# Squaring a softmax sum on ScalarE instead of GpSimd in a fused attention and SoLU feed-forward kernel

## The chip, the cores and the metric

One core of a Trainium2 chip runs the whole program. The metric is the device time of one execution in microseconds (us). A core has five engines with an instruction queue each: TensorE (PE in the profile, with its weight loads shown as PEld), VectorE (DVE), ScalarE (ACT), GpSimd (POOL) and SyncE (SP), which here only issues transfers.

## The reference

Two stages, with every product in float32. `q` is 4 x 12288 x 128; `kv` is 4 x 384 x 32 x 128 and is averaged over 4 x 4 blocks to 768 keys for each batch.

```python
kv_flat = kv_pool.reshape(B, -1, C) @ w_sr          # keys and values: 768 x 128
s = scale * (q @ k.transpose(0, 2, 1)); s = s - s.max(-1, keepdims=True)
a = np.exp(s); a /= a.sum(-1, keepdims=True) + 1e-09
x = a @ v                                           # tokens x 128
h = x @ w_in                                        # tokens x 1024
e = np.exp(h - h.max(-1, keepdims=True))
solu = h * (e / (e.sum(-1, keepdims=True) + 1e-09))
mu, var = solu.mean(-1), ((solu - mu) ** 2).mean(-1)
out = ((solu - mu) / np.sqrt(var + 1e-06) * g_ln) @ w_out
```

## The kernel before

The 49,152 tokens are 384 tiles of 128 (96 tiles to a batch), and four tiles make a group, so there are 96 groups. One loop runs over slots; slot `s` starts tile `s` and carries on older tiles at fixed distances, so that every engine's queue holds work of several tiles. From slot 9 to slot 389 the order of the instructions on each engine is the order in which the code writes them.

For tile `t` in its own slot `t`: TensorE makes the scores (L359) one slot ahead, VectorE takes the row maximum (L375), ScalarE takes the exponential (L376) and writes its float16 high part (L378), VectorE the low part (L386), and SyncE's queue issues a transposing transfer into `pT` (L389). A group's values are then multiplied (L412), read by ScalarE (L421, L422), and GpSimd makes the low part `xl` (L428). Ten slots behind, at `i = slot - 10`: TensorE makes `h` (L455), VectorE its maximum (L461), ScalarE the second exponential with its sum `z2` (L476). A slot later, for tile `i - 1`: VectorE makes `u` (L490), ScalarE the sum of squares `v3` (L521), GpSimd splits `u` into two float16 parts (L507, L508), and SyncE's queue issues the transposing transfer into `uT` (L513), which the output product (L540) reads two slots later. The scores and `h` share three PSUM buffers, so that TensorE's next scores (L359) wait for VectorE's `u`, and its next `h` for VectorE's low part of the scores.

Once for a group, in slot 4g + 15, `final_scale` makes the factor of the group's rows, (z2'^2 + v3)^(-1/2) for four tiles in one 128 x 4 tile, with z2' = (z2 + 1e-9) times a factor of the batch, `bb[:, 1:2]`. In that slot its code stands after ScalarE's L376 and L378 (tile `slot`) and before ScalarE's L521 (tile `slot - 11`) and GpSimd's L507 and L508 (the same tile). VectorE uses the factor two slots later (L564).

GpSimd has other work for a group: `ql` (L345), `xl` (L428), a sum (L435) whose reciprocal is VectorE's (L440), and, in the first three batches, the pooling of the next batch's keys: 30 additions of 128 x 384 (L201) in the slots 9 to about 67 of a batch, one to every second slot. In the rest of those batches a short series of steps makes the next batch's keys and values. The last batch has none of this. `kv_bound` runs once for a batch and fills `bb`.

Of the kernel before, what the change touches and what calls it, by code (L numbers as in the profile page):

```python
# [11 lines left out]
F32 = mybir.dt.float32  # L12
# [5 lines left out]
AF = mybir.ActivationFunctionType  # L18
ALU = mybir.AluOpType
# [33 lines left out]
def kernel(  # L53
# [15 lines left out]
    nc = tc.nc  # L69
# [52 lines left out]
    state = {}  # L122

    def kv_alloc(b):
        for n, w, dt, bufs in (
            ("kT", NK, F32, 1),
            ("ks", NK, F32, 1),
            ("kh", NK, F32R, 2),
            ("kl", NK, F32R, 2),
            ("ksq", NK, BF16, 1),  # L130
            ("kss", 2, F32, 1),
            ("knm", 2, F32, 1),
            ("vf", NK, F32, 1),
            ("sv", 2, F32, 2),
            ("bb", 2, F32, 2),
        ):
            state[n, b] = bat.tile([P, w], dt, tag=n, name=f"{n}_{b}", bufs=bufs)
        for n in ("vh", "vl"):
            state[n, b] = bat.tile([P, NKC, P], F16, tag=n, name=f"{n}_{b}")
# [125 lines left out]
    def kv_bound(b, part):  # L265

        knm, bb = state["knm", b], state["bb", b]
        if part == 0:
            nc.vector.tensor_tensor(bb[:, 0:1], knm[:, 0:1], knm[:, 1:2], op=ALU.max)
            nc.vector.tensor_scalar(  # L270
                bb[:, 0:1], bb[:, 0:1], wmax2, 1e-20, op0=ALU.mult, op1=ALU.max
            )
            nc.gpsimd.tensor_tensor(bb[:, 0:1], bb[:, 0:1], mhalf[:, 0:1], op=ALU.pow)
        else:
            nc.vector.tensor_scalar(
                bb[:, 1:2], bb[:, 0:1], SC * 1e-3 * 2.0**15, None, op0=ALU.mult
            )
            nc.vector.tensor_scalar(bb[:, 0:1], bb[:, 0:1], SC, None, op0=ALU.mult)

    def kv_vs(b, half):  # L280
        nc.scalar.activation(
            half_of("ks", b, half), half_of("kT", b, half), AF.Copy, scale=state["sv", b][:, 0:1]
        )
# [264 lines left out]
    def final_scale(g):  # L548

        b = g * GT // TPB  # L550
        f = grp.tile([P, GT], F32, tag="f", name=f"f_{g}")
        f2 = grp.tile([P, GT], F32, tag="f2", name=f"f2_{g}")
        nc.gpsimd.tensor_scalar(  # L553
            f, state.pop(("z2", g)), 1e-9, state["bb", b][:, 1:2], op0=ALU.add, op1=ALU.mult
        )
        nc.gpsimd.tensor_tensor(f2, f, f, op=ALU.mult)  # L556
        nc.gpsimd.tensor_tensor(f, f2, state.pop(("v3", g)), op=ALU.add)  # L557
        nc.gpsimd.tensor_tensor(f2, f, mhalf[:, :GT], op=ALU.pow)  # L558
        state["f", g] = f2
# [35 lines left out]
    nc.scalar.dma_start(wsr, w_sr)  # L595
    nc.scalar.mul(w_sr16, wsr, 1.0 / RR)
    kv_alloc(0)
    kv_first(0, (0, 1))
    raw_in = dmt.tile([P, 2 * DFF], I32, tag="pT", name="raw_in")
# [89 lines left out]
    def kv_norms(half):  # L689
# [9 lines left out]
        5: [w_center, partial(kv_norm_max, 0, 0)],  # L699
        6: [partial(kv_norm_max, 0, 1)],  # L700
        7: [w_square, partial(kv_bound, 0, 0)],
        8: [w_norm, partial(kv_bound, 0, 1)],
        9: [w_pow],
        10: [w_high],
# [17 lines left out]
        (93, 0, kv_norm_pe, kv_norm_out), (96, 0, kv_norm_max),  # L722
        (97, 1, kv_norm_pe, kv_norm_out), (99, 1, kv_norm_max),
        (103, 0, kv_bound), (104, 1, kv_bound),
    ]
    WITH_PE = {slot for slot, _, *fs in PLAN if len(fs) > 1}
# [15 lines left out]
    for slot in range(NT + LO + 2):  # L742
# [10 lines left out]
        if ti == 12 and tb + 1 < B:  # L753
            kv_alloc(tb + 1)
# [10 lines left out]
        at_last(slot - NORM, values_norm)  # L765
        at_last(slot - XSP - 1, values_split)
        at_last(slot - FSC, final_scale)
        if slot < NT and 0 < qs < slot and (slot - 1 - qs) % GT == 0:
            q_low(slot // GT + 1)
# [63 lines left out]
```

## Time before, and how its profile is read

| | us |
|---|---|
| median of the 3 runs | 1951.87 |
| lowest and highest run | 1951.87, 1959.1 |
| the profiled execution | 1954.76 |
| its span, first to last instruction | 1953.0 |

The span is what the views of the trace are drawn from; 1.76 us of the profiled execution lie around it. Five engines are each busy for 90% or more of the span. So a share of busy time alone doesn't tell which of them sets the pace: it has to be read stage by stage, from the gaps.

### The profile page before, as it was taken

The page shows a single profiled execution, that of the slowest core. Times are in us where ns is not written, and L with a number is a line of the kernel's source. Part 1 is how long each engine was busy: PE and PEld are TensorE (multiplying, and loading weights), DVE is VectorE, ACT ScalarE, POOL GpSimd, SP SyncE. Part 2 cuts the span into 40 slices and gives each one's busy share as a digit, 9 for nine tenths or more (in the row PEclk, how much of TensorE's full clock was granted, in tenths as well). Part 3 has the DMA queues.
Part 4 walks back from the last instruction along what each step waited for, and adds up shares of the span by engine and source line. Part 5 has one row for each costly group of instructions (what it writes and reads, how often), then busy time and mean ns, then how long its engine had stood idle before and what let it go on. Part 6 is the DMA issues. An engine that isn't in the chain of part 4 may idle for free. (4 is left out here: it accounts for less than half of the span.)

```text
span 1953.0 us, 43521 instructions
## 1 busy us (share of the span) xinstructions
PE 1899.8 (97%) x15678; PEld 1487.8 (76%) x15678; DVE 1797.4 (92%) x2573; ACT 1783.9 (91%) x3141; POOL 1760.0 (90%) x1579
## 2 busy tenths in 40 slices
PE   7999999999999999999999999999999999999997
PEld 4677777777777777777777777777777887787775
DVE  7899999999999999999999999899999999999985
ACT  3998999999999999999999999999999999999995
POOL 3699999999899999999989999999988898988886
PEclk8999999999999999999999999999999999999998
DMA  6899999999999999999999999999999999999996
GB/s 237 174 237 233 235 225 238 221 221 217 213 242 231 238 228 226 226 223 222 217 221 237 237 235 229 228 229 219 223 210 215 223 218 221 225 215 219 224 198 135
DMA packets 1484311, 432.88 MB, mean 222 GB/s; under 512 B 1405889, under 2 KB 1471553, under 8 KB 1483841
## 3 DMA queue, kind: packets, MB, share of 16 engines
q1 hardware_dynamic: 1469840, 410.10, 104.6%
q10 hardware_dynamic: 14256, 20.00, 3.9%
q8 instruction: 125, 2.05, 0.5%
q14 instruction: 90, 0.73, 0.1%
HBM read 52.50 MB, written 25.17 MB: 40 GB/s over the span
## 5 line engine op out<-in xcount | busy, mean ns | idle before, releaser
L508 POOL TENSOR_TENSOR uhl<-u,uhl 128x1024 f16<-128x1024 f32 x384 | 823.2, 2144 | 37.4 <-ACT uhl L505 6.0
L540 PEld LDWEIGHTS <-uT 128*128 128x128 f16 x9216 | 517.5, 98 | 112.8 <-issue 104.6
L540 PE MATMUL o<-wch,uT 128*128 128x128 f16 x6144 | 582.9, 220 | 7.2 <-DMA uT<-uhl 6.8
L540 PE MATMUL o<-wcl,uT 128*128 128x128 f16 x3072 | 536.0, 219 | 0.0
L490 DVE SCALAR_TENSOR_TENSOR u<-h,rz,e 128x1024 f32<-128x1024 f32 x384 | 490.2, 1277 | 24.9 <-ACT e L476 24.5
L461 DVE TENSOR_REDUCE nm<-h 128x1 f32<-128x1024 f32 x384 | 468.9, 1221 | 19.0 <-PE h L455 11.7
L476 ACT ACTIVATE e<-h,nm,rz 128x1024 f32<-128x1024 f32 x384 | 460.1, 1198 | 3.6 <-DVE rz L440 2.8
L521 ACT ACTIVATE junk<-u,su 128x1024 bf16<-128x1024 f32 x384 | 438.0, 1141 | 1.9 <-DVE u L490 1.9
L507 POOL TENSOR_SCALAR uhl<-u 128x1024 f16<-128x1024 f32 x378 | 395.9, 1047 | 10.4 <-DVE u L490 10.2
L412 PE MATMUL xa<-pT,vh 128*128 128x512 f16 x1152 | 391.5, 382 | 7.4 <-DMA pT<-phl 5.2
L375 DVE TENSOR_REDUCE nm<-s 128x1 f32<-128x768 f32 x384 | 365.3, 951 | 34.6 <-PE s L359 34.0
L376 ACT ACTIVATE s<-s,nm 128x768 f32<-128x768 f32 x384 | 335.7, 874 | 60.9 <-DVE nm L375 60.0
L386 DVE SCALAR_TENSOR_TENSOR phl<-s,phl 128x768 f16<-128x768 f32 x384 | 364.9, 951 | 20.0 <-ACT phl L378 10.5
L378 ACT ACTIVATE phl<-s 128x768 f16<-128x768 f32 x384 | 311.4, 811 | 12.0
L455 PE MATMUL h<-w_in_h,xh 128*128 128x512 f32 x768 | 304.9, 478 | 7.0 <-DVE phl L386 3.2
L359 PE MATMUL s<-kh,qh 128*128 128x384 f32 x768 | 264.4, 425 | 7.2 <-DVE u L490 2.8
L455 PE MATMUL h<-w_in_h,xl 128*128 128x512 f32 x768 | 245.1, 400 | 12.0 <-POOL xl L428 11.6
L455 PE MATMUL h<-w_in_l,xh 128*128 128x512 f32 x768 | 240.3, 394 | 0.0
L412 PE MATMUL xa<-pT,vl 128*128 128x512 f16 x576 | 219.1, 380 | 0.0
L359 PE MATMUL s<-kh,ql 128*128 128x384 f32 x768 | 196.2, 337 | 0.0
L359 PE MATMUL s<-kl,qh 128*128 128x384 f32 x768 | 196.1, 336 | 0.0
L455 PEld LDWEIGHTS h<-w_in_h,xh 128*128 128x128 f32 x768 | 140.4, 190 | 72.6 <-issue 18.2
(119 smaller groups left out, 2223.0 us busy)
## 6 DMA issues: line engine op xcount, KB each, us to landing
qf<-in_q_dram SPq DMA_DIRECT2D x96, 256.0 KB, 3.3
out_dram<-ob SPq DMA_DIRECT2D x96, 256.0 KB, 2.8
kv<-in_kv_dram ACTq DMA_DIRECT2D x96, 192.0 KB, 3.1
kv<-in_kv_dram SPq DMA_DIRECT2D x16, 384.0 KB, 7.8
pT<-phl SPq DMA_TRANSPOSE x384, 4.0
uT<-uhl SPq DMA_TRANSPOSE x384, 4.3
raw_in<-in_moe_w_in_dram ACTq DMA_DIRECT2D x1, 1024.0 KB, 6.5
raw_out<-in_moe_w_out_dram SPq DMA_DIRECT2D x1, 1024.0 KB, 7.6
```

Source lines behind the costliest of these rows:

```text
L359: nc.tensor.matmul(s[:, half, :384], lh[:, ts], rh[:, half * 384 : (half + 1) * 384], start=n == 0, stop=n == 2,)
L375: nc.vector.tensor_reduce(nm, s, axis=AX.XY, op=ALU.max, negate=True)
L386: nc.vector.scalar_tensor_tensor(phl[:, 1], state.pop(("s", t)), SC, phl[:, 0], op0=ALU.mult, op1=ALU.subtract)
L412: nc.tensor.matmul(xa, v[:, c, :], pT[:, :, a * NKC + c, :], start=n == 0, stop=n == len(seq) - 1)
L455: nc.tensor.matmul(h[:, hs], lh[:, ts], rh[:, hs], start=n == 0, stop=n == 2)
L461: nc.vector.tensor_reduce(nm[:, 0:1], state["h", t], axis=AX.X, op=ALU.max, negate=True)
L476: nc.scalar.activation(e, state["h", t], AF.Exp, bias=nm[:, 1:2], scale=state["rz", g][0][:, js], accum_out=state["z2", g][:, js],)
L490: nc.vector.scalar_tensor_tensor(u, state.pop(("h", t)), state["rz", g][1][:, j : j + 1], state.pop(("e", t)), op0=ALU.mult, op1=ALU.mult, ...
L507: nc.gpsimd.tensor_scalar(uhl[:, 0, :], u, 1.0, 1.0, op0=ALU.mult, op1=ALU.mult)
L508: nc.gpsimd.tensor_tensor(uhl[:, 1, :], u, uhl[:, 0, :], op=ALU.subtract)
L521: nc.scalar.activation(junk, u, AF.Square, scale=-float(DFF), bias=su, accum_out=state["v3", g][:, j : j + 1],)
L540: nc.tensor.matmul(po[:, ts], uT[:, a * NFC + c, :], w[:, c, :], start=c == 0 and n == 0, stop=c == NFC - 1 and n == 2,)
```

## The change

`bb` gets a third column, `bb[:, 1:2]` times 1e-9, made by one more VectorE instruction for a batch. In `final_scale` one ScalarE activation makes the square, (scale * z2 + bias)^2 with both scale and bias read from `bb`, in place of GpSimd's L553 (add and multiply) and L556 (the product with itself). GpSimd's L557 and L558 stay.

```diff
-            ("bb", 2, F32, 2),
+            ("bb", 3, F32, 2),
...
             nc.vector.tensor_scalar(bb[:, 0:1], bb[:, 0:1], SC, None, op0=ALU.mult)
+            nc.vector.tensor_scalar(bb[:, 2:3], bb[:, 1:2], 1e-9, None, op0=ALU.mult)
...
-        nc.gpsimd.tensor_scalar(
-            f, state.pop(("z2", g)), 1e-9, state["bb", b][:, 1:2], op0=ALU.add, op1=ALU.mult
-        )
-        nc.gpsimd.tensor_tensor(f2, f, f, op=ALU.mult)
+        bb = state["bb", b]
+        nc.scalar.activation(
+            f2, state.pop(("z2", g)), AF.Square, scale=bb[:, 1:2], bias=bb[:, 2:3]
+        )
         nc.gpsimd.tensor_tensor(f, f2, state.pop(("v3", g)), op=ALU.add)
         nc.gpsimd.tensor_tensor(f2, f, mhalf[:, :GT], op=ALU.pow)
```

## Rows read from the trace of the kernel before

**Rows 1.** The page's first part: busy time, share of the span, instructions

```profile
PE 1899.8 (97%) x15678; PEld 1487.8 (76%) x15678; DVE 1797.4 (92%) x2573; ACT 1783.9 (91%) x3141; POOL 1760.0 (90%) x1579
```

**Rows 2.** Two stretches: length, busy us of PE, PEld, DVE, ACT, POOL, then granted clock

```profile
600.00:840.00 240.00, 234.06 (x1951) 183.39 (x1950) 220.84 (x314) 222.06 (x392) 229.69 (x207) 1.00 1.13 231
...
1490.00:1758.00 268.00, 267.76 (x2269) 213.93 (x2268) 255.30 (x365) 254.70 (x449) 239.01 (x211) 1.00 1.13 220
```

**Rows 3.** Order of time on POOL, around one `final_scale` of batch 1, and the next

```profile
680.25 2.15 POOL L508 TENSOR_TENSOR uhl<-u,uhl 128x1024 f16<-128x1024 f32 x1
682.50 0.27 POOL L553 TENSOR_SCALAR f<-z,bb 128x4 f32<-128x4 f32 x1
682.85 0.20 POOL L556 TENSOR_TENSOR f<-f 128x4 f32<-128x4 f32 x1
683.13 0.20 POOL L557 TENSOR_TENSOR f<-f,v 128x4 f32<-128x4 f32 x1
...
702.34 0.27 POOL L553 TENSOR_SCALAR f<-z,bb 128x4 f32<-128x4 f32 x1
```

**Rows 4.** Waits of PE from 100 to 1880 us: total, times, longest

```profile
PE h L455 <- POOL xl L428: 10.9, 22, 1.4
PE xa L412 <- DMA pT<-phl: 5.0, 4, 2.2
PE s L359 <- DVE u L490: 1.8, 3, 0.6
PE xa L412 <- ACT phl L378: 1.1, 2, 0.8
```

**Rows 5.** Order of time on ACT: L521 of tiles 96, 124, 152, 288 and 344

```profile
543.95 1.14 ACT L521 ACTIVATE junk<-u,su 128x1024 bf16<-128x1024 f32 x1
...
680.15 1.14 ACT L521 ACTIVATE junk<-u,su 128x1024 bf16<-128x1024 f32 x1
...
820.68 1.14 ACT L521 ACTIVATE junk<-u,su 128x1024 bf16<-128x1024 f32 x1
...
1491.28 1.14 ACT L521 ACTIVATE junk<-u,su 128x1024 bf16<-128x1024 f32 x1
...
1759.20 1.14 ACT L521 ACTIVATE junk<-u,su 128x1024 bf16<-128x1024 f32 x1
```

**Rows 6.** Groups by line: busy us, mean ns, idle before

```profile
L441 ACT ACTIVATE rz<-rz,bb 128x4 f32<-128x4 f32 x96 | 28.1, 293 | 2.6 <-DVE rz L440 2.6
...
L619 ACT ACTIVATE wsq<-top_in 128x1024 bf16<-128x1024 f32 x1 | 1.1, 1052 | 0.0
...
L275 DVE TENSOR_SCALAR bb<-bb 128x1 f32<-128x1 f32 x4 | 0.6, 147 | 0.7 <-POOL bb L273 0.7
```

**Rows 7.** Order of time on ACT in the last batch, around one `final_scale`

```profile
1529.39 1.14 ACT L521 ACTIVATE junk<-u,su 128x1024 bf16<-128x1024 f32 x1
...
1530.58 1.21 ACT L476 ACTIVATE e<-h,nm,rz 128x1024 f32<-128x1024 f32 x1
...
1532.27 0.88 ACT L376 ACTIVATE s<-s,nm 128x768 f32<-128x768 f32 x1 [0.39 <-DVE nm L375]
...
1542.03 0.29 ACT L441 ACTIVATE rz<-rz,bb 128x4 f32<-128x4 f32 x1
1542.21 0.61 ACT L337 CAST qh<-qf 128x512 fp32r<-128x512 f32 x1
```

**Rows 8.** Order of time on DVE, the same stretch

```profile
1532.15 1.28 DVE L490 SCALAR_TENSOR_TENSOR u<-h,rz,e 128x1024 f32<-128x1024 f32 x1
```

**Rows 9.** Order of time on POOL, the same stretch

```profile
1529.05 0.20 POOL L557 TENSOR_TENSOR f<-f,v 128x4 f32<-128x4 f32 x1
...
1538.17 1.27 POOL L428 TENSOR_TENSOR xl<-xf,xh 128x512 fp32r<-128x512 f32 x1 [1.06 <-ACT xf L422]
```

**Rows 10.** Order of time on PE, the same stretch

```profile
1534.73 0.70 PE L359 MATMUL s<-kh,qh 128*128 128x384 f32 x2
...
1542.21 0.63 PE L455 MATMUL h<-w_in_h,xl 128*128 128x512 f32 x2
```

## The prediction, as it went on record before the changed kernel ran

> **What bounds the kernel now.** The page's first part comes first: five engines stand between 90 and 97% of the span [rows 1]. That ranking alone says nothing on a change that takes work from POOL (90%) and gives it to ACT (91%), so I asked for busy time by stretch. The reader is to see in it that the kernel has two regimes. In the last batch, from 1490 to 1758 us, PE is busy for 267.76 of 268 us at the full granted clock, and POOL for 239.01 (89%). In batch 1, from 600 to 840 us, PE falls to 234.06 of 240, and POOL rises to 229.69 (95.7%) [rows 2]. What POOL has there on top is the pooling of the next batch's keys.
>
> Is the missing 4.3% of POOL idle time in which something could go? The order of time on POOL says no. Its instructions of 0.20 to 0.27 us start 0.27 to 0.35 us apart, with no wait noted, and the next group's L553 comes 702.34 - 682.50 = 19.84 us later [rows 3]. So 19.84 us a group is POOL's own serial time there: the rest is the small step between two instructions. The order of time on ACT gives the other regime. L521 of tiles 96 and 152 start 276.73 us apart, those of tiles 288 and 344, at the same place of the last batch, 267.92 us: for 14 groups that is 19.77 against 19.14 us a group [rows 5]. The first agrees with POOL's 19.84, the second with a PE without gaps. POOL sets the pace where it pools keys, and PE elsewhere.
>
> The waits show who pays. From 100 to 1880 us PE waited 10.9 us, 22 times, for POOL's `xl`, 5.0 us for the transfers into `pT`, and 1.1 us for ACT's `phl` [rows 4]. All of these lie in the pooling stretches. The transfers belong to the same case: they are issued in order on SP behind L513, which waits for POOL's L508.
>
> **The change, part by part.**
>
> *POOL loses L553 and L556.* From L553's start to L557's is 683.13 - 682.50 = 0.63 us [rows 3], so a group costs POOL 19.84 - 0.63 = 19.21 us. That is just above PE's 19.14 [rows 5]. POOL's excess over PE, 0.70 us a group, shrinks to 0.07, over the 14 groups to 1 us, and POOL's queue can run that far behind before PE feels it: in the last batch `xl` ends at 1538.17 + 1.27 = 1539.44 and PE wants it at 1542.21, 2.8 us later [rows 9, 10].
>
> *What that is worth* is bounded from two sides. From above: the whole difference of pace, 276.73 - 267.92 = 8.8 us a batch, less about 0.6 for the one key product that falls in this window and which PE does anyway, is 8.2 for batches 1 and 2, and some 6.5 for batch 0, whose pooling starts in the start-up: 22.9 us. From below: only the waits that name `xl`, 10.9 us [rows 4]. In between stand all PE waits of that kind, 10.9 + 5.0 + 1.1 = 17.0 us. Weight loads that start late add a little to that, so I take 18 us, nearer to the wait rows than to the pace, since a small residue stays where a batch's longest POOL steps fall.
>
> *ACT gets one activation for a group.* The trace has no 128 x 4 Square with two operands from SBUF. The nearest is L441, 128 x 4 with one: 293 ns busy [rows 6], and the next instruction starts 0.18 us behind its start [rows 7]. What a further operand costs is seen between L619, a Square of 1024 columns with none, 1052 ns [rows 6], and L521, the same with a bias, 1.14 us [rows 5]: 0.09 us. So 0.18 to 0.27 us of ACT's time, and I take 0.27; for 96 groups 17 to 26 us. It does not reload a table: Square (L521) and Exp (L476) already alternate without one [rows 7]. What hides it: the next tile's `u` on VectorE. L476 ends at 1530.58 + 1.21 = 1531.79 and L490 starts only at 1532.15, 0.36 us later; ACT itself then waits 0.39 us for VectorE (L376) [rows 7, 8]; and after `u` ends at 1533.43, PE takes its buffer at 1534.73, 1.3 us later [rows 10]. I cost it at nothing. With the cover gone it is those 26 us.
>
> The Trainium skill (Perfetto Trace Analysis, Identifying the Most-Contended Engine) speaks against the change: among VectorE, ScalarE and GpSimd the engine with the highest occupancy is the one to relieve, and by the page's shares that is VectorE, then ScalarE, so an instruction moved to ScalarE would buy nothing or cost its 26 us. The stretches of [rows 2] disagree with using the whole span's shares, for POOL is highest, 229.69 against 222.06 and 220.84, just where PE loses time.
>
> *A new wait.* L557 waited for ACT's `v3`, a slot old; now it also waits for the Square, which is queued behind L376 and L378 of the same slot and just ahead of the L521 of [rows 5, 7]. In a pooling stretch POOL comes late: the Square would start at 680.15 and be done by 680.6, and POOL arrives at 682.50 [rows 3, 5]: no wait. In the last batch POOL comes early: the Square would start at 1529.39, where L521 stands now [rows 7], and end 0.38 us (293 ns and the operand) later at 1529.77; L557 started at 1529.05 [rows 9], so it moves by about 0.8 us. Behind it on POOL are L558, two tiles' L507 and L508, and then L428, which waits 1.06 us for ACT anyway [rows 9]: the 0.8 us fit. The two tiles' transfers into `uT` go out later on SP by up to 0.8 us, with the next `pT` behind them; PE waits for neither in that batch, so I cost this at nothing too. If it is not hidden, it costs up to 0.8 us in some 45 groups.
>
> *VectorE gets one instruction for a batch*, like L275, 147 ns [rows 6]: 0.6 us in all at most, nothing at least; I take nothing. ACT's `z2` buffer is no longer held by POOL, which frees nothing that the trace shows a wait for. At the end of the program POOL's two instructions go too, in a stretch where its chain counts: under 1 us, left out.
>
> *The sum:* 1954.76 - 18 = 1936.8 for the profiled execution. That one is 2.9 us above the median of the runs, 1951.87, so on that scale it is 1933.9, or 1934. The forecast's own range, with 11 to 23 us, is 1929 to 1941.
>
> **The rivals.**
>
> *Half of it lands on the next bound.* After the change POOL's 19.21 and PE's 19.14 us a group are level, and ACT has one more instruction; two chains of equal length that wait for each other run slower than either. If half of the 0.63 us is given back as waits of ACT and VectorE on each other, 9 us stay, or 5 to 9: 1943 to 1947. For it: ACT's waits for VectorE show that these two are never far apart [rows 7]. Against it: PE runs without gaps at 19.14 in the last batch with the same chains.
>
> *Nothing is freed.* If L557 finds the Square unfinished in the pooling stretches as well, POOL's wait takes the place of its work: 1950 to 1954. It needs POOL to run more than 2 us earlier there than now [rows 3, 5], and it can't, since its 19.21 us a group still fill PE's pace.
>
> *ACT is exposed: slower.* The Square delays L476, `u`, and PE's scores. It decides from 0.36 us on [rows 7, 8], where the 0.18 to 0.27 us no longer fit in front of `u`, and PE's reserve behind must be gone as well. Then 96 groups pay 0.27 us, 26 us, against the 18 gained: 1951.9 + 8 = 1960; without the gain 1978. By the rule of the skill above this is the case to expect; the trace's own reserves are against it.
>
> **How the numbers follow.** A difference under 0.5% (9.8 us) can hardly be told from no change here. The forecast has 72%, half of it 13%, nothing freed 7%, ACT exposed 8%. The forecast lies below 1942 (1951.87 less 0.5%): faster 0.72. The next two are within 0.5%: 0.20. ACT exposed 8 us or more: slower, 0.08. The range reaches from the most that the pace could give, 1951.9 - 23 and 2 for the end of the program and the spread of the runs, 1926, up over the rival of half the gain to where nothing is freed, 1950.
>
> **What would show it.** Right: PE's waits for `xl` in the pooling stretches go from 10.9 us to under 3, those for `pT` too; tiles 96 and 152 stand about 268.5 us apart instead of 276.73, while tiles 288 and 344 stay at 268; POOL's busy time falls by some 45 us (96 times 0.27 + 0.20), ACT's grows by 26 or more; the Square takes about 0.38 us and the next L521 starts 0.27 us behind it; in the last batch POOL waits at L557 for ACT. Wrong: waits of PE for VectorE's `u` or `phl` in the last batch, a pace there above 19.14 us a group, or pooling stretches in which POOL waits for ACT at L557.

## The result: 16 us faster, and the profile after

The changed kernel took 1936.66 us (median of 4 runs, 1935.16 to 1938.33) against 1952.65 us for the kernel before: the ratio is 0.9911, with a 95% interval of [0.9888, 0.9934], so 0.9% or 16 us faster. In a second measurement, beside the last experiments below, the ratio was 0.9922, [0.9906, 0.9938]. The forecast was 1934 us, 18 us faster. The profiled execution took 1936.14 us with a span of 1934.1 us. In the code of after every line behind L279 stands one line further down: the scores are L360, the sum of squares L522, the Square L555, GpSimd's two remaining steps L558 and L559.

Busy time of all engines over the span:

```profile
PE 1894.0 (98%) x15677; PEld 1488.8 (77%) x15678; DVE 1803.1 (93%) x2577; ACT 1800.8 (93%) x3237; POOL 1712.8 (89%) x1387
```

POOL lost 192 instructions and 47 us, ACT gained 96 and 17 us [rows 1]. By stretch, in the columns of [rows 2] (behind the granted clock, 1.00, stand the share of time in which the DMA engines were busy and the GB/s that they moved):

```profile
600.00:840.00 240.00, 239.57 (x2024) 190.68 (x2022) 226.63 (x323) 229.91 (x415) 230.34 (x188) 1.00 1.19 237
1490.00:1758.00 268.00, 267.54 (x2267) 213.72 (x2266) 255.96 (x364) 257.44 (x464) 231.94 (x183) 1.00 1.09 221
```

In the pooling stretch PE went from 234.06 to 239.57 of 240 us: it now runs there as densely as in the last batch, and does 2024 matmuls in the time in which it did 1951 (the two windows are the same times, not quite the same tiles). POOL is as busy as before (230.34), but with the work of more tiles. In the last batch PE is the same and only POOL is less busy.

PE's waits from 100 to 1860 us are the lines that answer to [rows 4]:

```profile
PE s L360 <- DVE u L491: 2.4, 6, 0.6
PE xa L413 <- ACT junk L522: 1.5, 1, 1.5
PE xa L413 <- ACT phl L379: 1.0, 1, 1.0
...
PE xa L413 <- DMA pT<-phl: 0.4, 1, 0.4
```

The 22 waits for `xl` are gone (10.9 us), and of the 5.0 us for `pT` 0.4 is left under that name. In the order of time on ACT, the sums of squares of tiles 96, 152, 288 and 344, as in [rows 5]:

```profile
539.93 1.14 ACT L522 ACTIVATE junk<-u,su 128x1024 bf16<-128x1024 f32 x1
...
809.35 1.14 ACT L522 ACTIVATE junk<-u,su 128x1024 bf16<-128x1024 f32 x1
...
1473.01 1.14 ACT L522 ACTIVATE junk<-u,su 128x1024 bf16<-128x1024 f32 x1
...
1740.92 1.14 ACT L522 ACTIVATE junk<-u,su 128x1024 bf16<-128x1024 f32 x1
```

Tiles 96 and 152 now stand 809.35 - 539.93 = 269.42 us apart, 276.73 before; tiles 288 and 344 1740.92 - 1473.01 = 267.91, 267.92 before. The whole difference of the two spans, 18.9 us, can be laid out in this way, from the starts of the same ACT instruction:

| from tile to tile | before, us | after, us | difference |
|---|---|---|---|
| 0 to 56 (pooling) | 275.30 | 270.70 | -4.6 |
| 56 to 96 | 196.90 | 197.83 | +0.9 |
| 96 to 152 (pooling) | 276.73 | 269.42 | -7.3 |
| 152 to 192 | 197.02 | 197.66 | +0.6 |
| 192 to 248 (pooling) | 276.70 | 268.75 | -8.0 |
| 248 to 288 | 196.88 | 197.25 | +0.4 |
| 288 to 344 (last batch) | 267.92 | 267.91 | 0.0 |

The three pooling stretches give 19.9 us, the stretches behind them take 1.9 back, and start and end give about 0.9. Each number is one execution's: the changed kernel profiled a second time has 270.6, 268.8 and 271.0 us in the three pooling stretches, so a single stretch of one kernel can differ by 2 us and more.

On POOL, around one of its two remaining steps in a pooling stretch, and the next:

```profile
652.47 2.14 POOL L509 TENSOR_TENSOR uhl<-u,uhl 128x1024 f16<-128x1024 f32 x1
654.63 0.20 POOL L558 TENSOR_TENSOR f<-f,v 128x4 f32<-128x4 f32 x1
...
673.74 0.20 POOL L558 TENSOR_TENSOR f<-f,v 128x4 f32<-128x4 f32 x1
```

A group takes 19.11 us, against 19.84 [rows 3] and against the 19.21 that was worked out. On ACT the Square of that group stands like this:

```profile
654.18 0.38 ACT L555 ACTIVATE f<-z,bb 128x4 f32<-128x4 f32 x1
654.46 1.14 ACT L522 ACTIVATE junk<-u,su 128x1024 bf16<-128x1024 f32 x1
```

It ends at 654.56, and POOL, free at 652.47 + 2.14 = 654.61, starts L558 at 654.63. The two meet. In the kernel before, POOL came about 2 us behind that point of ACT.

### The profile page after: what moved, and what is told of

The parts are those of the page before. It is cut to its first block, busy times and chain, and to the rows that moved or that the text cites. A ratio compares the mean times of both kernels' runs of the same rounds, so it can differ in the third digit from the quotient of the medians.

```text
span 1934.1 us, 43332 instructions
## 1 busy us (share of the span) xinstructions
PE 1894.0 (98%) x15677; PEld 1488.8 (77%) x15678; DVE 1803.1 (93%) x2577; ACT 1800.8 (93%) x3237; POOL 1712.8 (89%) x1387
## 5 line engine op out<-in xcount | busy, mean ns | idle before, releaser
L491 DVE SCALAR_TENSOR_TENSOR u<-h,rz,e 128x1024 f32<-128x1024 f32 x384 | 491.2, 1279 | 32.6 <-ACT e L477 30.4
L522 ACT ACTIVATE junk<-u,su 128x1024 bf16<-128x1024 f32 x384 | 437.7, 1140 | 1.6 <-DVE u L491 1.6
L508 POOL TENSOR_SCALAR uhl<-u 128x1024 f16<-128x1024 f32 x378 | 394.8, 1044 | 8.1 <-DVE u L491 7.9
L376 DVE TENSOR_REDUCE nm<-s 128x1 f32<-128x768 f32 x384 | 365.3, 952 | 28.3 <-PE s L360 27.6
L377 ACT ACTIVATE s<-s,nm 128x768 f32<-128x768 f32 x384 | 335.5, 874 | 31.2 <-DVE nm L376 30.7
L360 PE MATMUL s<-kh,qh 128*128 128x384 f32 x768 | 264.0, 424 | 7.4 <-DVE u L491 3.4
L360 PE MATMUL s<-kh,ql 128*128 128x384 f32 x768 | 196.0, 337 | 0.0
L360 PE MATMUL s<-kl,qh 128*128 128x384 f32 x768 | 195.5, 335 | 0.0
```

The lines of the kernel that those rows point to most:

```text
L360: nc.tensor.matmul(s[:, half, :384], lh[:, ts], rh[:, half * 384 : (half + 1) * 384], start=n == 0, stop=n == 2,)
L376: nc.vector.tensor_reduce(nm, s, axis=AX.XY, op=ALU.max, negate=True)
L491: nc.vector.scalar_tensor_tensor(u, state.pop(("h", t)), state["rz", g][1][:, j : j + 1], state.pop(("e", t)), op0=ALU.mult, op1=ALU.mult, ...
L508: nc.gpsimd.tensor_scalar(uhl[:, 0, :], u, 1.0, 1.0, op0=ALU.mult, op1=ALU.mult)
L522: nc.scalar.activation(junk, u, AF.Square, scale=-float(DFF), bias=su, accum_out=state["v3", g][:, j : j + 1],)
```

## The experiments

All were timed against the kernel before on the same chip; ratios are to that. "Pooling" is the mean over the three pooling stretches of the table above, "behind" that over the three stretches that follow them, "last" the stretch of tiles 288 to 344, all from one profiled execution (before: 276.2, 196.9 and 267.9; after: 269.6, 197.6 and 267.9).

| kernel | median us | ratio, 95% interval | pooling | behind | last |
|---|---|---|---|---|---|
| GpSimd less, ScalarE as before | 1933.7 | 0.9887 [0.987, 0.9904] | 269.8 | 196.7 | 267.9 |
| ScalarE more, GpSimd as before | 1955.54 | 1.0004 [0.9995, 1.0012] | 276.4 | 197.2 | 267.9 |
| changed, GpSimd's time put back | 1952.73 | 0.9991 [0.9982, 1.0] | 275.7 | 197.1 | 267.9 |
| before, GpSimd's time doubled | 1982.34 | 1.014 [1.0126, 1.0154] | 285.1 | 197.9 | 268.0 |
| changed, half put back | 1941.36 | 0.9936 [0.9923, 0.9949] | 270.7 | 197.7 | 267.9 |
| changed, without the power | 1934.67 | 0.9895 [0.9876, 0.9913] | 269.5 | 196.7 | 267.9 |
| changed, Square a slot early | 1932.79 | 0.9901 [0.9886, 0.9917] | 268.7 | 197.6 | 267.9 |
| the same again | 1935.04 | 0.9907 [0.9893, 0.9921] | 269.1 | 197.6 | 267.9 |
| the changed kernel again | 1940.97 | 0.9922 [0.9906, 0.9938] | 270.1 | 197.6 | 267.9 |
| both on VectorE | 1951.94 | 0.999 [0.9981, 0.9999] | 273.4 | 199.1 | 268.0 |
| changed, two Squares | 1946.27 | 0.9952 [0.9935, 0.997] | 273.0 | 198.0 | 268.0 |
| early Square, last batch's products spread | 1934.94 | 0.9905 [0.9889, 0.992] | 270.2 | 197.5 | 267.4 |

**GpSimd less, ScalarE as before.** The square is left out of the factor: a constant stands in its place.

```diff
-        nc.gpsimd.tensor_scalar(
-            f, state.pop(("z2", g)), 1e-9, state["bb", b][:, 1:2], op0=ALU.add, op1=ALU.mult
-        )
-        nc.gpsimd.tensor_tensor(f2, f, f, op=ALU.mult)
-        nc.gpsimd.tensor_tensor(f, f2, state.pop(("v3", g)), op=ALU.add)
+        state.pop(("z2", g))
+        nc.gpsimd.tensor_tensor(f, onesm[:, :GT], state.pop(("v3", g)), op=ALU.add)
```

> The kernel before with GpSimd's two instructions taken out and nothing put on ScalarE; the square is left out of the factor, and a constant is added to v3 in its place. If GpSimd's serial time in the pooling stretches is what the change relieved, and ScalarE's activation costs nothing, this is as fast as the changed kernel: 1935 to 1938 us. If ScalarE's activation costs something that hides part of the gain, this is faster than the changed kernel, down to 1930 us, where the difference of pace is recovered in full. If the gain came from the new wait or the new order and not from GpSimd's time, it stays near 1953 us.

1933.7 us: removing the two instructions alone gives the whole gain and perhaps 3 us more than the change (the intervals, [0.987, 0.9904] and [0.9888, 0.9934], overlap). So the new wait and the new order aren't what brought it, and ScalarE's activation costs little.

**ScalarE more, GpSimd as before.** The Square is made into a tile that nobody reads.

```diff
+        bb = state["bb", b]
+        sq = grp.tile([P, GT], F32, tag="sq", name=f"sq_{g}")
+        nc.scalar.activation(
+            sq, state["z2", g], AF.Square, scale=bb[:, 1:2], bias=bb[:, 2:3]
+        )
         nc.gpsimd.tensor_scalar(
             f, state.pop(("z2", g)), 1e-9, state["bb", b][:, 1:2], op0=ALU.add, op1=ALU.mult
```

> The kernel before with ScalarE's Square added and its result unused; GpSimd keeps both instructions. Activation hidden: 1952 to 1955 us. Activation exposed on the way from the scores to u: 96 times 0.27 us, up to 1979 us.

The ratio is 1.0004: hidden, in the pooling stretches and in the last batch (267.9 us). ACT's busy time grows by 24.3 us, and its idle time in front of the scores' exponential (L376, here L377) falls from 60.9 to 40.6 us: that is, most of the Square's time seems to come out of ACT's waits for VectorE.

**GpSimd's time put back into the changed kernel, and doubled in the kernel before.** Both add these lines in front of the rest of `final_scale`:

```diff
+        d = grp.tile([P, GT], F32, tag="d", name=f"d_{g}")
+        d2 = grp.tile([P, GT], F32, tag="d2", name=f"d2_{g}")
+        nc.gpsimd.tensor_scalar(
+            d, onesm[:, :GT], 1e-9, state["bb", b][:, 1:2], op0=ALU.add, op1=ALU.mult
+        )
+        nc.gpsimd.tensor_tensor(d2, d, d, op=ALU.mult)
```

> The changed kernel with two GpSimd instructions of the same form and size put back at the same place, on a constant and without any wait for ScalarE. GpSimd's serial time is the cause: back to 1951 to 1956 us, tiles 96 and 152 about 276 us apart. The cause is the square's new place, its wait, or the z2 buffer that GpSimd no longer holds: it stays at 1937 us.

> The kernel before with two further GpSimd instructions of that form for a group. GpSimd's serial time sets the pace in some 14 to 16 groups of each of three batches: 0.63 us for each, 26 to 30 us, so 1979 to 1983 us, and the last batch keeps its 268 us between tiles 288 and 344. GpSimd not the bound: 1953 to 1956 us.

The changed kernel with the time put back is the kernel before, 0.9991, although the square is still ScalarE's and GpSimd holds no `z2`. Its waits of PE show the old cause again:

```profile
PE h L456 <- POOL xl L429: 8.9, 19, 1.3
```

Doubled, it is 28 us slower, and the waits for `xl` grow from 10.9 to 36.3 us:

```profile
PE h L455 <- POOL xl L428: 36.3, 36, 2.0
```

The pooling stretches are 8.8 us longer than before, 14 groups by 0.63 us each, and the last batch is as it was: it has GpSimd time to spare. The stretches behind the pooling are 0.9 us longer, 10 groups each, so GpSimd's time counts a little there too.

**Half put back.** The changed kernel with one of the two, the product, put back on a constant (`nc.gpsimd.tensor_tensor(d2, onesm[:, :GT], onesm[:, :GT], op=ALU.mult)`).

> The changed kernel with one GpSimd instruction of 0.28 us put back for a group, on a constant. GpSimd's serial time is the cause, and the gain grows with each tenth of it until TensorE's pace is reached: 1941 to 1946 us. If only the removal of both counts (a step, not a slope): 1937 or 1953 us.

1941.36 us, 0.6% below the kernel before, so half of the time doesn't cost the whole gain. Against the changed kernel (0.9911 [0.9888, 0.9934] and 0.9922 [0.9906, 0.9938]) the interval [0.9923, 0.9949] overlaps: whether the half costs anything, and so whether it is a slope, isn't shown by this run.

**Without the power.** The inverse square root is left out of the factor.

```diff
         nc.gpsimd.tensor_tensor(f, f2, state.pop(("v3", g)), op=ALU.add)
-        nc.gpsimd.tensor_tensor(f2, f, mhalf[:, :GT], op=ALU.pow)
-        state["f", g] = f2
+        state["f", g] = f
```

> The changed kernel with GpSimd's L559 taken out too, 1.0 us more for a group; the inverse square root is left out of the factor. If TensorE sets the pace everywhere once GpSimd is below it, the further 1.0 us bring almost nothing: 1931 to 1937 us. If GpSimd still sets the pace somewhere, as the 0.63 us did: 10 to 20 us faster, 1916 to 1926 us.

1.0 us less on GpSimd for each group, more than the change removed, brings nothing that can be told from the changed kernel (0.9895 [0.9876, 0.9913] against 0.9911 [0.9888, 0.9934]). The gain ends where the change ends: behind it stands PE, which in the pooling stretch is as dense as in the changed kernel, while POOL falls to 217.49 us:

```profile
600.00:840.00 240.00, 239.56 (x2024) 190.84 (x2023) 226.97 (x323) 229.95 (x416) 217.49 (x176) 1.00 1.20 238
```

**The Square a slot early.**

```diff
-        nc.scalar.activation(
-            f2, state.pop(("z2", g)), AF.Square, scale=bb[:, 1:2], bias=bb[:, 2:3]
-        )
...
+        at_last(slot - FSC + 1, final_square)
         at_last(slot - FSC, final_scale)
```

`final_square` holds the tile `f2` and the same activation.

> The changed kernel with ScalarE's Square issued one slot earlier, so that GpSimd finds it finished. If GpSimd's 80.6 us of waiting for the Square in the changed kernel are idle time that nobody needs, nothing changes: 1934 to 1939 us, with the wait gone from GpSimd's list. If that wait still costs something, this is faster than the changed kernel: 1928 to 1933 us.

> The Square one slot early again, now beside the changed kernel on one chip. If the one or two waits of TensorE for pT that the changed kernel's profile still shows depend on GpSimd's wait for the Square, 2 to 4 us faster than the changed kernel; if they are chance, the same within 1.5 us.

GpSimd's wait for the Square, 77.8 us between 100 and 1860 us in the changed kernel, is gone, and as much turns up as longer waits for other things (the two below were 1.0 and 9.9 us in the changed kernel):

```profile
POOL uhl L508 <- DVE u L491: 43.2, 51, 1.4
POOL xl L429 <- ACT xf L423: 40.8, 54, 1.4
```

The time is 1932.79 and, beside the changed kernel on one chip, 1935.04 against 1940.97 us. The intervals of the ratios, [0.9893, 0.9921] and [0.9906, 0.9938], overlap: this version is at least as good as the changed one, and that it is better isn't shown.

**Both on VectorE.** The kernel before with `nc.vector` in place of `nc.gpsimd` for L553 and L556.

> The kernel before with the two instructions on VectorE in place of GpSimd, nothing on ScalarE. If only relieving GpSimd counts and VectorE's reserve takes two short instructions: 1934 to 1941 us. If the engine with the highest busy share of the whole span is the bound, and that is VectorE, its 0.2 to 0.3 us a group come on top: 19 to 29 us slower than with GpSimd relieved, 1955 to 1966 us.

1951.94 us: 0.1% below the kernel before, so nearly all of the gain is lost, but not as either expectation had it. VectorE's time in the last batch is hidden as well (268.0 us). The pooling stretches take 273.4 us, 3.8 more than in the changed kernel, and the stretches behind them 199.1, 1.5 more. The order of time on DVE in a pooling stretch:

```profile
678.33 0.62 DVE L553 TENSOR_SCALAR f<-z,bb 128x4 f32<-128x4 f32 x1
678.99 0.16 DVE L556 TENSOR_TENSOR f<-f 128x4 f32<-128x4 f32 x1
679.07 1.22 DVE L461 TENSOR_REDUCE nm<-h 128x1 f32<-128x1024 f32 x1
```

and on POOL at that place:

```profile
676.78 2.15 POOL L508 TENSOR_TENSOR uhl<-u,uhl 128x1024 f16<-128x1024 f32 x1
679.30 0.20 POOL L557 TENSOR_TENSOR f<-f,v 128x4 f32<-128x4 f32 x1 [0.37 <-DVE f L556]
```

VectorE's two steps cost 679.07 - 678.33 = 0.74 us and not 0.2 to 0.3. The first of them starts while GpSimd's L508 runs and ends with it (676.78 + 2.15 = 678.93 against 678.33 + 0.62 = 678.95), and then GpSimd, which has hardly any time to spare here, waits 0.37 us for the second. 19.11 + 0.37 = 19.48 us a group is close to the pace of this kernel, 273.4 / 14 = 19.53. PE's waits name VectorE's `phl` too, 5.4 us from 100 to 1880 us; how much of the loss is GpSimd's wait and how much VectorE's own time wasn't taken apart.

**Two Squares.** The changed kernel with a second Square in front of the first, into a tile that nobody reads.

> The changed kernel with a second Square of the same form, its result unused. If ScalarE's cover in front of u (0.36 us in the kernel before, of which one Square took 0.28) is what hides the activation, the second one reaches VectorE's u but stops at TensorE's reserve behind it: at most 3 us slower, 1936 to 1941 us. If ScalarE's time counts in full: 96 times 0.28, 27 us slower, 1963 us.

By the ratios, 0.9952 [0.9935, 0.997] against 0.9922 [0.9906, 0.9938] for the changed kernel beside it, it is 6 us slower, where at most 3 were expected; the intervals overlap at their ends, so the size is uncertain. The last batch has 268.0 us, so there a second Square is hidden too. Nearly all of the loss lies in the pooling stretches (273.0 against 270.1). POOL's noted waits for the Square in these stretches are 14.8 us in 16 of 41 groups, against 4.1 us in 7, and VectorE's `u` waits 18.8 us for GpSimd over the whole program, against 1.4. The longer wait may thus be the cause. But `u` waits for GpSimd in the last batch as well, 14 times and 3.4 us, and nothing is lost there; and ScalarE's own time is a rival. A version with two Squares and no wait wasn't run, so the cause stays open.

**The last batch's products.** In the last batch PE sets the pace, and some of its groups are 0.54 us longer than their neighbours (19.65 against 19.11 us). The guess was that the values products leave room there for key work that this batch doesn't have.

```diff
-        if g > 1 and {first % TPB, first % TPB + TPB} & WITH_PE:
+        if g > 1 and first < NT - TPB + 9 and {first % TPB, first % TPB + TPB} & WITH_PE:
```

> The Square one slot early, and in the last batch the values products of a group are spread 4, 5, 5, 4 over the slots everywhere, not 0, 6, 6, 6 in the slots in which the other batches have key work. If TensorE alone sets the pace there, each of the five groups that this touches gains the 0.54 us by which it is longer than its neighbours (19.65 against 19.11): 2 to 3 us faster than the Square one slot early. If something else made those groups longer: the same.

> The changed kernel again, beside the three below on one chip: 1934 to 1938 us.

The groups of 19.6 us, one in the stretch of tiles 288 to 344 and two close behind it, take 19.1 in this version's trace, which bears the guess out, and the stretch is 267.4 against 267.9 us. The time is the same as without (0.9905 against 0.9907): too small to be told from the runs' spread. The changed kernel itself came out at 1940.97 us here, 3 us above what was expected, 1932.2 to 1943.69.

## Why the prediction was right, step by step

**Two regimes, and POOL the bound in one.** Right, and shown: time put back on POOL restores the old time, doubled time costs 0.63 us in 14 groups of each of the first three batches, and whatever was added to or taken from POOL, ACT or VectorE, the last batch stays at 267.9 to 268.0 us.

**POOL's serial time a group.** 19.21 us was worked out; 19.11 is the distance from group to group in the trace, the same as between most groups of the last batch, where PE sets the pace. It is a pace, and POOL's own time can be that or less. So POOL is no longer behind.

**What that is worth.** 18 us were chosen between bounds of 10.9 and 22.9: the 17.0 us of waits, and a little for weight loads. In the profile the pooling stretches gave 19.9 and the stretches behind them took 1.9 back, which the sum didn't have; with 0.9 at start and end, left out of the sum as small, the spans differ by 18.9. The medians differ by 16, within the spread of the runs. The waits of the three kinds fell from 17.0 us to 2.9 (counting that of `xa` for `junk` among them), and PE's busy time fell by 5.8 us [rows 1], where the sum had allowed 1. So the two terms were off in opposite directions, and that the total came out within 2 us owes something to luck. Half of the gain, 1943 to 1947 us, is excluded by the first measurement (1935.16 to 1938.33); the second, up to 1943.69, comes near it.

**ACT's activation at nothing.** Nearly. It takes 0.38 us and the next instruction starts 0.28 us behind its start, against an estimate of 0.27. ACT's busy time grew by 17 us where 26 or more were named as a sign; with the Square alone added to the kernel before it was 24.3. The last batch, 267.91 against 267.92 us, hides it fully, by the cover that was named: L491 starts at 1532.74 there, behind the end of the exponential at 1532.54, and ACT's own wait shrank from 0.39 to 0.19 us:

```profile
1531.35 1.19 ACT L477 ACTIVATE e<-h,nm,rz 128x1024 f32<-128x1024 f32 x1
...
1532.83 0.88 ACT L377 ACTIVATE s<-s,nm 128x768 f32<-128x768 f32 x1 [0.19 <-DVE nm L376]
```

On DVE at that place:

```profile
1532.74 1.28 DVE L491 SCALAR_TENSOR_TENSOR u<-h,rz,e 128x1024 f32<-128x1024 f32 x1
```

Whether ScalarE's time costs something in the stretches behind the pooling, which took 1.9 us back in all, isn't settled. They are 196.9 us each in the kernel before (the mean of the three), 197.2 with the Square added to it, 197.6 in the changed kernel, and 196.7 in the changed kernel without the power. The last of these has the Square too, so it is not ScalarE's time alone: GpSimd's 1.0 us less a group took 0.9 us off such a stretch.

**The new wait in the pooling stretches.** This is the step that failed. It said that POOL would come 2 us after the Square and couldn't run earlier. POOL did run earlier, by all of those 2 us, until it met the Square (654.61 against 654.56). In 27 of the 41 groups of the three pooling stretches L558 starts 0.08 us behind the end of the Square, just as in all 14 groups of the last batch between tiles 288 and 344, so there the wait sets when POOL goes on; only seven of these waits are long enough to be noted, 3.3 us in all. So a sign of being wrong came up, and with it the condition of the rival by which nothing is freed. Its price, 1950 us or more, did not: PE's waits for `xl` are gone all the same, and a version without the wait gains nothing that could be shown. In the last batch POOL waits as foretold, and longer than the 0.8 us by which L557 was to move, because the 0.63 us of removed work are idle now too:

```profile
1530.40 0.20 POOL L558 TENSOR_TENSOR f<-f,v 128x4 f32<-128x4 f32 x1 [1.54 <-ACT f L555]
```

From 100 to 1860 us such waits are 77.8 us in 55 groups; in the last batch they cost nothing (267.9 us before and after).

**The rival from the occupancy rule** (Perfetto Trace Analysis, Identifying the Most-Contended Engine, in the Trainium skill: relieve the engine with the highest occupancy). By shares of the whole span it would have spoken for VectorE or ScalarE, and by the prediction for up to 26 us more. The runs disagree with the rule used in that way and agree with it used by stretch: POOL's 229.69 of 240 us marked the bound.

## What to carry to other kernels

Where five engines are all above 90% busy, compare two stretches of the same work: the one with a leaner queue shows what the next bound is, and the difference of pace is the most that a change can give. An engine whose short instructions follow each other at 0.27 to 0.35 us without a noted wait was full here at 96% busy. When work is moved from a full engine to another, the wait for its result replaces the work as soon as the engine catches up, so look how early the moved step can be issued.

## What the runs showed of the hardware that was not expected

VectorE's 128 x 4 add-and-multiply (L553 of the version with both steps on VectorE) took 223 to 1874 ns in the same program, median 227, mean 415, where GpSimd needs 269 to 273 for it. The spread follows GpSimd. Of the 96, 56 took 223 to 228 ns. The 40 longer ones all started while a GpSimd TENSOR_TENSOR ran (37 times L508, three times L223, 128 x 384), and all ended 22 to 32 ns behind its end: the VectorE instruction didn't finish before GpSimd's was done. So the version on VectorE made GpSimd wait for a step that had itself been held up by GpSimd. The kernel before has it too: L269, a 128 x 1 product on VectorE, took 146 ns once and 1667 to 1669 ns three times, ending 12 to 14 ns behind the end of an L508. It isn't every VectorE instruction: the two row maxima (L375, L461) and `u` (L490), 384 each, stay within 3% of their median. The Trainium skill (GPSIMD Engine Reference, Specifications) says that GpSimd shares its SBUF interfaces with VectorE, with contention for certain VectorE instructions. The trace agrees with that; what sets these instructions apart wasn't tested.
